# Which tiles of a head pair are turned on TensorE: three and three, or two and four

## Chip, cores and metric

The kernel runs on one core of a Trainium2 chip. The metric is the device time of one execution in microseconds; several executions are timed and their median is given. One further execution is profiled, and its trace is what the prediction reads.

## What is computed

Three layers follow each other, on 2 batches of 768 rows:

1. Attention with 8 heads of width 64. Query and key rows are hashed into 64 buckets by the signs of 6 projections; a score counts only where the buckets agree.
2. A mixing layer, `u = x + (x^T U V)^T` along the rows, then `u + relu(u w_ch1) w_ch2` with widths 512, 2048, 512.
3. Four causal attention experts of width 64, of which each row takes the best two by a gate.

```python
scores = np.where(mask, scale * q @ k.T, -1e9)
attn = softmax(scores); x = attn @ v            # layer 1, per head
u = x + (x.T @ U @ V).T
x = u + np.maximum(u @ w_ch1, 0) @ w_ch2        # layer 2
```

## The kernel before

All three layers are cut into tiles of 128 rows. The change touches layer 1 of batch 0 alone. There the 8 heads are worked off as 4 pairs (pair 0 to 3 below), each pair as two heads of six row tiles; the twelve tiles of a pair are numbered 0 to 11 here, 0 to 5 in the first head, 6 to 11 in the second (`a1_head`). Each tile goes through these steps:

- TensorE makes 128 x 768 scores in PSUM (L606, L611); VectorE copies them out as `P32` with their least value (L617); ScalarE takes the exponential with the row sum (L526, or L575 in the other mode).
- Then the 128 x 768 weights must be turned, so that TensorE can multiply them with the values, and there are two ways. In mode `AP` (`softmax_split`) ScalarE writes a half-precision copy (L528), GpSimd writes the remainder (L534), and the SyncE queue issues one DMA transposition of both halves into the buffer `PT` (L628); TensorE then makes 18 half-precision multiplications (L538 to L540). In mode `FAV` (`softmax_f32`) TensorE turns the float32 weights itself, six blocks in two halves (L581); ScalarE copies one half to SBUF (L586) and VectorE the other (L588), and six float32 multiplications follow, which the trace shows as 12 passes (L590). No DMA takes part.
- When all six tiles of a head have been multiplied, VectorE scales the result into `xn` (L639). The result lies in one PSUM buffer (`po`, tag `pv`, one buffer), so a second head's first product waits for that.

`A1_MODES[b][p]` is the list of modes of a pair; tile `NT * j + t` takes entry `(NT * j + t) % len(list)`. `P32`, `PT` and the half-precision buffer `HL` are rings of five buffers in batch 0. Tiles of batch 1 are all `AP` in pair 0, `AP` and `AV` in turn after that.

What lies around it in the same stretch: while a pair runs, the next pair is prepared (`a1_prep`: GpSimd makes `KN` and `KL`, L409 and L414; the SyncE queue issues three transpositions `AQ`, `AK`, `KT`, L407 to L418, and copies `BQ`, `BK`, L419, L421; the signs follow six tiles later, with four small DMAs, L446, L447); the pair after that is loaded (L381); the weights of layer 2 are loaded and split in 512-column units (L278, then L189 to L195 on VectorE, L281 on ScalarE, L282 and L283 on GpSimd); and the pair before goes through the row mixing of layer 2 (`x_stage_a` to `x_stage_c`, L657 to L683), from which the multiplications of layer 2 (L734, L754) start once batch 0 is complete.

All DMAs are issued from one queue, SyncE's, in order. The order on each engine is not written by hand: a planner places the instructions by priorities (the order of the program, moved by `sooner`) and by a time model of its own.

Of the kernel before, what the change touches and what calls it, by code (L numbers as in the profile page):

```python
# [22 lines left out]
def kernel(  # L23
# [28 lines left out]
    NP = H // 2  # L52
# [8 lines left out]
    CLIP = 8e9  # L61
    WPOOL = True
    A1_MODES = (
        [("AP", "FAV")] * NP,
        [("AP",)] + [("AP", "AV")] * (NP - 1),
    )
    A2_MODES = ("AV", "VP")
# [1137 lines left out]
```

## Time and profile before

| | us |
|---|---|
| median of 3 executions | 636.69 (635.64 to 643.04) |
| profiled execution, its own time | 635.59 |
| its span, first to last instruction | 633.8 |
| TensorE matmul busy | 579.1 (91%) |
| VectorE, ScalarE, GpSimd busy | 422.7, 348.5, 232.1 |

The profiled execution's own time is the one to add to; 1.8 us of it lie outside the span. Busy time is an average over stretches with different limits: batch 0 of layer 1 fills about 18 to 161 us, batch 1 of layer 1 up to about 365 us with layer 2 beside it, and the rest is layers 2 and 3.

### The profile page before, as it was taken

What the parts mean: (1) busy time and instruction counts of PE and PEld (TensorE: products, weight loads), DVE (VectorE), ACT (ScalarE), POOL (GpSimd) and SP (SyncE); (2) the same over time, 40 slices, a digit from 0 to 9 for tenths busy, and PEclk for the clock granted to TensorE, in tenths of its full rate; (3) what the DMA queues carried; (4) which work ended last, traced back from release to release, by engine and by line L of the source; (5) the groups of instructions that cost most, each with busy time, mean ns of one, the idle gap of its engine ahead of it and who ended that gap; (6) DMA issues with size and microseconds to landing.
All of it is one profiled execution on the core that took longest, in us unless ns stands there. A gap on an engine that the chain in (4) does not pass through costs nothing.

```text
span 633.8 us, 16209 instructions
## 1 busy us (share of the span) xinstructions
PE 579.1 (91%) x6498; PEld 477.0 (75%) x6498; DVE 422.7 (67%) x1029; ACT 348.5 (55%) x744; POOL 232.1 (37%) x218
## 2 busy tenths in 40 slices
PE   5698888978798799989999999999999999998995
PEld 3376866757577589875888898878887888997963
DVE  6989696988877863674876555583784435465295
ACT  4769485775786652673776543462453413344273
POOL 4738777686897662231432101020040000002021
PEclk9679797889889999999999999999999999999998
DMA  8799999999989999597587602242263102016064
GB/s 234 140 218 215 243 211 244 227 228 269 219 182 251 231 178 172 101 200 114 108 130 121 101 20 50 38 84 72 46 114 67 34 15 39 27 35 109 23 107 109
DMA packets 228029, 84.36 MB, mean 133 GB/s; under 512 B 207057, under 2 KB 223473, under 8 KB 227953
## 3 DMA queue, kind: packets, MB, share of 16 engines
q1 hardware_dynamic: 227952, 83.32, 65.4%
q8 instruction: 51, 0.84, 0.6%
q14 instruction: 26, 0.20, 0.1%
HBM read 29.11 MB, written 3.15 MB: 51 GB/s over the span
## 4 chain that ended last, share of the span: by engine, by line
PE 59%; DMA 14%; DVE 7%; POOL 7%; ACT 6%; issue 5%; SPq 1%; POOLq 0%; DVEq 0%; ACTq 0%
PE px L754 18%; PE ph L734 12%; DMA PT<-HL 8%; PE po L590 3%; POOL HL L534 3%; PE pq L805 3%; PE s L908 2%; PE pk L805 2%; PE pz L1040 2%; PE pv L837 2%; ACT HL L528 2%; DVE P L617 2%; ACT P L526 2%; DMA more_hT<-more_W 2%; DMA more_hT<-HL 2%
## 5 line engine op out<-in xcount | busy, mean ns | idle before, releaser
L534 POOL TENSOR_TENSOR HL<-P,HL 128x768 f16<-128x768 f32 (+5 forms) x62 | 88.7, 1432 | 323.2 <-DVE HL L530 148.7
L734 PE MATMUL ph<-U,W 128*128 128x256 f16 (+1 forms) x1344 | 145.1, 258 | 1.7 <-DVE hT L736 1.1
L754 PE MATMUL px<-hT,W 128*128 128x256 f16 (+1 forms) x1344 | 146.1, 258 | 0.1
L734 PEld LDWEIGHTS <-W 128*128 128x128 f16 x1344 | 114.2, 98 | 17.1 <-issue 2.4
L754 PEld LDWEIGHTS <-W 128*128 128x128 f16 x1344 | 115.0, 98 | 14.3 <-issue 2.0
L526 ACT ACTIVATE P<-P,m 128x768 f32<-128x768 f32 (+5 forms) x109 | 88.7, 814 | 56.0 <-DVE P L916 28.7
L617 DVE TENSOR_SCALAR_CACHE_REDUCE P<-sc 128x768 f32<-128x768 f32 x76 | 71.9, 950 | 12.8 <-PE sc L611 8.4
L736 DVE SCALAR_TENSOR_TENSOR hT<-ph,hT 128x256 f16<-128x256 f32 (+1 forms) x112 | 42.6, 382 | 45.6 <-ACT hT L735 44.9
L528 ACT ACTIVATE HL<-P 128x768 f16<-128x768 f32 (+5 forms) x80 | 60.5, 758 | 17.6 <-DMA PT<-HL 14.8
L735 ACT ACTIVATE hT<-ph 128x256 f16<-128x256 f32 (+1 forms) x112 | 38.7, 347 | 51.3 <-PE ph L734 47.8
L538 PEld LDWEIGHTS <-PT 128*128 128x128 f16 x516 | 47.8, 99 | 23.8 <-DMA PT<-HL 20.1
L606 PE MATMUL sc<-AK,AQ 128*128 128x512 f16 x192 | 50.0, 341 | 9.3 <-DVE P L617 6.5
L538 PE MATMUL po<-V,PT 128*128 128x64 f16 x372 | 45.7, 195 | 11.5 <-DMA PT<-HL 10.6
L611 PE MATMUL sc<-BK,BQ 88*128 88x512 f16 x192 | 49.9, 340 | 0.0
L539 PEld LDWEIGHTS <-PT 128*128 128x128 f16 x516 | 47.5, 99 | 1.5 <-issue 0.2
L540 PEld LDWEIGHTS <-PT 128*128 128x128 f16 x516 | 47.4, 99 | 0.4
L540 PE MATMUL po<-V,PT 128*128 128x64 f16 x372 | 45.7, 195 | 0.0
L539 PE MATMUL po<-V,PT 128*128 128x64 f16 x372 | 45.2, 195 | 0.0
L534 DVE TENSOR_TENSOR HL<-P,HL 128x768 f16<-128x768 f32 (+5 forms) x42 | 32.3, 769 | 15.4 <-ACT HL L528 14.8
L916 DVE TENSOR_SCALAR_CACHE_REDUCE P<-s 128x128 f32<-128x128 f32 (+5 forms) x48 | 29.5, 618 | 10.9 <-PE s L913 10.6
L606 PEld LDWEIGHTS <-AQ 128*128 128x128 f16 x192 | 18.0, 105 | 17.8 <-issue 13.2
L611 PEld LDWEIGHTS <-BQ 88*128 88x128 f16 x192 | 19.5, 102 | 13.9 <-issue 2.1
(240 smaller groups left out, 1186.7 us busy)
## 6 DMA issues: line engine op xcount, KB each, us to landing
w<-in_moe_w_ch_dram SPq DMA_DIRECT2D x16, 512.0 KB
wx<-in_moe_w_ch_dram SPq DMA_DIRECT2D x16, 512.0 KB
qn<-in_q_dram SPq DMA_DIRECT2D x16, 192.0 KB
kn<-in_k_dram SPq DMA_DIRECT2D x16, 192.0 KB
vn<-in_v_dram SPq DMA_DIRECT2D x16, 192.0 KB
out_dram<-o SPq DMA_DIRECT2D x12, 256.0 KB
PT<-HL SPq DMA_TRANSPOSE x101
BQ<-AQ SPq DMA_DIRECT2D x7, 192.0 KB
```

The source lines that it names most:

```text
L526: nc.scalar.activation(P32, P32, AF.Exp, bias=m, scale=-1.0, accum_out=ssum)
L528: nc.scalar.activation(HL[:, 0], P32, AF.Copy)
L534: eng.tensor_tensor(HL[:, 1], P32, HL[:, 0], op=ALU.subtract)
L538: nc.tensor.matmul(o, PT[:, t, :], vh(t), start=(t == 0), stop=False)
L539: nc.tensor.matmul(o, PT[:, t, :], vl(t), start=False, stop=False)
L540: nc.tensor.matmul(o, PT[:, nk + t, :], vh(t), start=False, stop=(t == nk - 1))
L606: nc.tensor.matmul(ps[:, c0 : c0 + cn], aq[:, t, :], ak[:, c0 : c0 + cn], start=True, stop=False,)
L611: nc.tensor.matmul(ps[:, c0 : c0 + cn], bq[:, t, :], bk[:, c0 : c0 + cn], start=False, stop=True,)
L617: nc.vector.tensor_scalar(P32, ps[:, 0:S], CLIP, None, op0=ALU.min, op1=ALU.min, accum_out=m)
L734: nc.tensor.matmul(ph, w, u, start=(i == 0), stop=(i == len(ops) - 1))
L736: nc.vector.scalar_tensor_tensor(hT[1][:, ft, :], ph, 0.0, hT[0][:, ft, :], op0=ALU.max, op1=ALU.subtract)
L754: nc.tensor.matmul(po, w, u, start=(i == 0), stop=(i == len(ops) - 1))
```

## The change

Batch 0's list of modes gets twelve entries in place of two. Before, tiles 1, 3, 5 (first head) and 7, 9, 11 (second head) are `FAV`; after, tiles 2, 5 and 6, 8, 9, 11. Tiles 1, 3 and 7 change from `FAV` to `AP`, tiles 2, 6 and 8 from `AP` to `FAV`. It applies to all four pairs of batch 0; batch 1 stays.

```diff
     A1_MODES = (
-        [("AP", "FAV")] * NP,
+        [("AP", "AP", "FAV") * 2 + ("FAV", "AP", "FAV") * 2] * NP,
         [("AP",)] + [("AP", "AV")] * (NP - 1),
     )
```

## Rows read from the trace of the kernel before

**Rows 1.** The page: TensorE's busy time, granted clock and DMA share in 40 slices.

```profile
PE 579.1 (91%) x6498; PEld 477.0 (75%) x6498; DVE 422.7 (67%) x1029; ACT 348.5 (55%) x744; POOL 232.1 (37%) x218
...
PEclk9679797889889999999999999999999999999998
DMA  8799999999989999597587602242263102016064
```

**Rows 2.** Windows: busy time of each engine, clock, DMA share; pair 2, then layers 2 and 3.

```profile
84.00:122.00 38.00, 33.24 (x336) 27.23 (x334) 30.55 (x63) 26.87 (x52) 27.80 (x25) 0.87 1.10 228
...
365.00:634.00 269.00, 257.24 (x3022) 220.52 (x3020) 149.99 (x492) 111.76 (x307) 28.76 (x29) 0.99 0.29 58
```

**Rows 3.** Groups of instructions by line and form: count, busy us, mean ns.

```profile
L534 POOL TENSOR_TENSOR HL<-P,HL 128x768 f16<-128x768 f32 x42 | 69.5, 1656 | 97.5 <-ACT HL L528 89.7 <-DVE ss L1013 3.1 <-DVE mx L869 2.9
L528 ACT ACTIVATE HL<-P 128x768 f16<-128x768 f32 x60 | 50.2, 838 | 16.7 <-DMA PT<-HL 14.8 <-DMA more_hT<-HL 1.0
...
L588 DVE COPY PT<-tp 128x384 f32<-128x384 f32 x14 | 7.7, 548 | 2.6 <-PE tp L581 2.6
L586 ACT ACTIVATE PT<-tp 128x384 f32<-128x384 f32 x14 | 6.6, 473 | 0.6 <-PE tp L581 0.6
```

**Rows 4.** Chain of waits, in order of time, pair 2: start us, us, what.

```profile
97.87 4.96 DMA PT<-HL
...
106.34 0.05 PE po L538
...
107.31 2.61 PE po L590 x12
109.92 1.28 PE tp L581 x6
...
121.43 1.37 PE po L590 x12
```

**Rows 5.** Timeline of SyncE's queue, end of pair 1 to end of pair 3.

```profile
81.31 0.39 SPq L278 DMA_DIRECT2D w<-in_moe_w_ch_dram  x1
82.41 1.47 SPq L628 DMA_TRANSPOSE more_hT<-more_W  x1
...
88.31 1.92 SPq L407 DMA_TRANSPOSE AQ<-QN  x1
...
97.87 1.47 SPq L628 DMA_TRANSPOSE PT<-HL  x1
...
101.23 1.75 SPq L628 DMA_TRANSPOSE more_hT<-HL  x1
...
104.91 3.37 SPq L628 DMA_TRANSPOSE PT<-HL  x1
...
113.72 1.50 SPq L628 DMA_TRANSPOSE more_hT<-more_W  x1
115.33 0.81 SPq L278 DMA_DIRECT2D wx<-in_moe_w_ch_dram  x1
119.06 2.41 SPq L628 DMA_TRANSPOSE PT<-more_W  x1
...
158.01 3.72 SPq L407 DMA_TRANSPOSE AQ<-QN  x1
161.83 1.29 SPq L628 DMA_TRANSPOSE PT<-HL  x1
```

**Rows 6.** Timeline of VectorE, pair 2: tiles 7 and 8 leave PSUM.

```profile
101.48 0.94 DVE L617 TENSOR_SCALAR_CACHE_REDUCE more_W<-sc 128x768 f32<-128x768 f32 x1
...
114.41 0.96 DVE L617 TENSOR_SCALAR_CACHE_REDUCE P<-sc 128x768 f32<-128x768 f32 x1 [0.96 <-PE sc L611]
```

**Rows 7.** Windows of 2 us, pair 2: columns as in rows 2.

```profile
100.00:102.00 2.00, 0.20 (x2) 0.00 (x0) 2.00 (x5) 1.72 (x4) 2.00 (x2) 1.00 1.21 176
...
104.00:106.00 2.00, 2.00 (x14) 2.00 (x14) 0.00 (x0) 0.00 (x0) 2.00 (x2) 0.50 1.17 285
```

**Rows 8.** Timeline of GpSimd, pair 2: the remainder of tile 8.

```profile
117.39 1.64 POOL L534 TENSOR_TENSOR more_W<-P,more_W 128x768 f16<-128x768 f32 x1 [0.80 <-ACT more_W L528]
```

## Prediction

> **What bounds the kernel now.** I read the page first. TensorE is busy 91% of the span, but that is an average: the granted clock falls again and again in the first third, and the DMA engines are taken nine tenths or more in most slices there [rows 1]. Next the windows by stage. In pair 2 no engine is full: TensorE 33.2 of 38 us, part of it at half clock, VectorE 30.6, GpSimd 27.8, while the DMA share is 1.10, over one, so transfers queue behind each other. From 365 us on TensorE works 257 of 269 us and the DMA share is 0.29 [rows 2]. So batch 0 is a stretch of transfers and waits, everything behind it is TensorE's, and since the multiplications of layer 2 start when batch 0 is done, a microsecond won or lost in batch 0 reaches the end whole, unless the planner finds room for it.
>
> Then the timelines of one pair, pair 2. Its transpositions on SyncE's queue stand at 97.87, 101.23, 104.91, 113.72, 119.06 and a sixth later, for tiles 0, 2, 4, 6, 8, 10; ahead of the first stand the three of the next pair's preparation, from 88.31 on [rows 5]. TensorE runs dry while it waits for the first: 0.20 us busy in 100 to 102. Right after it the clock is 0.50 [rows 7], that is 1.2 GHz in place of 2.4, and the backlog is worked off slowly: the chain has a tile's 12 passes at 2.61 us there, against 1.37 us later [rows 4]. Tile 8's scores stand behind that backlog in TensorE's order, so VectorE, which took tile 7 at 101.48, gets tile 8 at 114.41 [rows 6]. This stop of 13 us in the middle of the pair is what the change can touch; pairs 1 and 3 show the same pattern.
>
> **The change part by part.** Counts first. Six tiles of a pair are turned by DMA and six on TensorE before and after, so no engine's work changes: the sum of removed and added instructions is nothing, for all four pairs. What is left is where they stand. Per pair the first head gets one DMA tile more and one TensorE tile less, the second head the reverse.
>
> One tile changed from TensorE to DMA, in the first head:
> - GpSimd gets a remainder of 1.66 us, ScalarE a copy of 0.84 for one of 0.47, so 0.37 more; VectorE loses a copy of 0.55 [rows 3].
> - TensorE at half clock loses 12 passes of 2.61 us and six turns of 1.28, and gets 18 multiplications at 0.05, so 3.89 less 0.90, or 3.0 us; at full clock about half, 1.5 us [rows 4].
> - SyncE's queue gets a transposition. Two of them follow each other at 3.36 and 3.68 us, the loads between them included [rows 5]; the chain shows 4.96 us from issue to the waiting multiplication [rows 4].
>
> The second head has each of these with the other sign. GpSimd, ScalarE and VectorE have gaps in either head (27.8, 26.9 and 30.6 of 38 us [rows 2]), so I cost them at nothing. That cover is thinnest on GpSimd, which is full in both windows of [rows 7] (2.00 of 2.00 us); without it the 1.66 us would show in each pair.
>
> Two things are left that can show.
>
> First, **the middle of the pair**. Tile 4, the last DMA tile of the first head, goes from third to fourth place among the pair's transpositions. The first head's result must be scaled out before the second head's products may start (one PSUM buffer), so they wait for it. The cost is between nothing and one pitch: nothing if the planner puts the fourth right behind the third and the half-clock backlog hides it (TensorE has 1.5 to 3.0 us less to do by then); 3.7 us if all of it is waited for. If the fourth kept its present slot, it would be 8.8 us behind the third (113.72 less 104.91 [rows 5]), but what lies between is loads and small copies that the planner is free to put behind it. I take half a pitch, 1.85 us.
>
> Second, **the fifth transposition**. It belongs to tile 8 now and to tile 7 after. In pair 2 the queue is free at 116.14 (115.33 and 0.81) and issues it at 119.06 [rows 5], the moment the remainder of tile 8 is done (117.39 and 1.64 [rows 8]). Tile 7 was scored 13 us earlier [rows 6], so its transposition would not wait. The gain is 2.92 us in pair 2, but 0.71 in pair 1 (81.70 to 82.41) and 0.10 in pair 3 (161.73 to 161.83 [rows 5]): mean 1.2 us, ends 0 and 2.9. After the fifth as many tiles are served as before (tiles up to 9), and after the sixth all, so nothing else is won or lost at the end of a pair.
>
> Net 1.85 less 1.2, or 0.65 us later per pair. Pair 0 is prepared in another way and I leave it out; three pairs give 2.0 us. 635.59 and 2.0 is 637.6 us against the profiled execution's own time. That execution lies 1.1 us under the median of the three runs shown, so I give **638 us**.
>
> The clock needs a word of its own. In this trace each dry spell of TensorE is followed by a stretch at half clock [rows 7]. The Trainium skill says the same in "TensorE: Matmul & The Clock Gate", section "HAM oscillation — how this bites in real kernels": bursts that wait for a transfer between them lose the clock and run at half rate. By that rule the change works against itself, since it puts four waits for transfers in the first head in place of three; the trace agrees as far as it goes, and the rival below prices it.
>
> **Rivals.** *Slower: the fourth transposition is waited for in full, and TensorE goes cold longer.* Place: the multiplications of tile 4, before the second head's first product. Price: one pitch of 3.7 us and no gain at the fifth, in four pairs 14.8 us, so 650 us; it decides where TensorE's first-head work (two TensorE tiles in place of three) no longer bridges the time between transpositions. For it: TensorE is already dry ahead of the first one. Against it: after that spell TensorE is the late one, not the queue, until tile 8's scores.
>
> *Faster: the second head no longer waits.* With two DMA tiles instead of three there, the fifth transposition issues 2.9 us sooner in every pair and the fourth hides in the backlog: four times 2.9 is 11.7, so 624 us. If in addition the half-clock stretch were shortened by one tile's difference (2.61 less 1.37, 1.2 us), it would be 5 us less again, 619. For it: the 13 us stop is mainly TensorE's backlog at half clock. Against it: two of the three pairs show a wait of under 1 us at the fifth.
>
> *The planner moves other work.* Its order over all engines depends on the modes, and the change may shift weight loads or the mixing step by a transposition's pitch, in either direction: one pitch of 3.7 us, so 632 or 640. That the change does nothing is excluded; each tile reads its mode from the list.
>
> **How the numbers follow.** The forecast with the planner's shifts (630 to 645 us) gets 0.78, the slower rival 0.12, the faster 0.10. The range, from 628 to 648, leaves out the outer half of both rivals. A change of 2% is about what a measurement of this kernel tells from none; that is 12.7 us, so faster means under 624.0 and slower over 649.4. The faster rival stands at the first bound and the slower just over the second, so each gives about half its chance, and a little falls to worse shifts: faster 0.06, within 2% 0.86, slower 0.08.
>
> **What would show it.** In the changed trace the transpositions of a pair belong to tiles 0, 1, 3, 4, 7, 10. Right: tile 4's is issued later in the pair than 20 us after tile 0's score, the fifth follows the fourth without a wait for GpSimd, and the pair's length stays within 2 us of 38. Wrong to the slow side: TensorE's half-clock stretch, 10 us in pair 2 now, grows. Wrong to the fast side: the stop between tiles 7 and 8 shrinks by several us and layer 2's first multiplication comes earlier. The forecast fails altogether if the end moves while layer 2 starts at the same time, since then the cause lies behind batch 0.

## The result, and the profile after

The changed kernel takes 641.14 us (median of 20 runs, 637.07 to 642.86) where the kernel before took 635.75 (20 runs, 630.91 to 643.04) on the same chip: ratio 1.0086, 95% interval 1.0066 to 1.0105. So it is slower by some 5 us, less than the 2% that the chances were given for, within the range and on the forecast's side, but not where the forecast put it. The profiled execution took 638.57 us, 3.0 more than that of before, and is the one that the rows show; of the 5.4 us between the medians they can account for these 3.0.

The page and the windows first, columns as in [rows 1, 2]; the second window is the first head of batch 1.

```profile
PE 577.7 (91%) x6498; PEld 469.7 (74%) x6498; DVE 421.6 (66%) x1029; ACT 347.7 (55%) x744; POOL 232.8 (37%) x218
...
84.00:122.00 38.00, 32.83 (x345) 25.91 (x344) 32.80 (x63) 28.74 (x53) 29.23 (x26) 0.96 1.05 228
171.79:197.17 25.38, 23.07 (x250) 16.39 (x249) 16.74 (x31) 17.45 (x34) 18.28 (x17) 0.80 0.95 189
```

Against [rows 1] TensorE's multiplications have 1.4 us less, the other engines differ by about 1 us at most. Pair 2 even runs at 0.96 of the clock where it ran at 0.87 [rows 2]. No work was added, so the end must have moved by order.

Where it moved is seen from VectorE's scaling of each head's result (L639). Its timeline in the changed kernel, pair 3 and batch 1's first head.

```profile
157.30 0.56 DVE L639 TENSOR_TENSOR xn<-po,r 128x384 f32<-128x384 f32 x1 [1.06 <-PE po L590]
...
171.79 0.56 DVE L639 TENSOR_TENSOR xn<-po,r 128x384 f32<-128x384 f32 x1 [2.46 <-PE po L590]
...
197.17 0.56 DVE L639 TENSOR_TENSOR xn<-po,r 128x384 f32<-128x384 f32 x1 [3.35 <-PE po L540]
```

The same line in both traces, with the time since the head before:

| result (L639) | before, us | after, us | head took before | after | difference |
|---|---|---|---|---|---|
| pair 0, second head | 59.73 | 56.76 | | | -2.97 |
| pair 1, first | 80.11 | 84.39 | 20.38 | 27.63 | +7.25 |
| pair 1, second | 94.70 | 97.05 | 14.59 | 12.66 | -1.93 |
| pair 2, first | 117.22 | 118.28 | 22.52 | 21.23 | -1.29 |
| pair 2, second | 133.31 | 131.78 | 16.09 | 13.50 | -2.59 |
| pair 3, first | 150.65 | 157.30 | 17.34 | 25.52 | +8.18 |
| pair 3, second | 173.15 | 171.79 | 22.50 | 14.49 | -8.01 |
| batch 1, first head | 190.98 | 197.17 | 17.83 | 25.38 | +7.55 |

Over pairs 1 to 3 first heads lose 14.1 us and second heads win 12.5; pair 0 wins 3.0, and batch 0 ends 1.4 us earlier. Layer 2's first multiplication is 1.2 us earlier too (177.35 to 176.13). (Batch 0 ends with pair 3's second head, at 173.15 us in the kernel before, and not at about 161.) Then one head of batch 1, whose modes were not touched, takes 7.6 us more. From there on nothing else is lost on balance: layer 3 begins at 371.6 us instead of 367.0, and from it to the end of the span it is 265.3 us against 266.8.

One trace of each kernel doesn't carry all of this. In three versions below (signs_whole, small_loads_after, mixing_later) the order on every engine is that of the changed kernel through batch 0. Batch 0 ends in them at 171.4, 175.4 and 175.1 us. In small_loads_before, which has the order of the kernel before up to some 160 us, pair 3's first result comes at 147.5 us instead of 150.65. So batch 0 moves by 3 to 4 us from one execution to the next, and that it ends 1.4 us earlier is not shown. What all four traces of the new order show is the shape: the first heads of pairs 1 and 3 take 26.2 to 27.6 and 25.3 to 25.7 us (20.4 and 17.3 before), that of pair 2 20.9 to 21.3 (22.5), every second head is shorter, and batch 1's first result comes at 197.2 to 198.9 us instead of 191.0.

SyncE's queue tells what stands between the transpositions of that head. The changed kernel, from the end of pair 2 to the middle of batch 1's first pair, columns as in [rows 5]:

```profile
117.37 0.51 SPq L381 DMA_DIRECT2D vn<-in_v_dram  x1
118.01 2.06 SPq L628 DMA_TRANSPOSE more_hT<-more_W  x1
...
136.72 1.49 SPq L628 DMA_TRANSPOSE more_hT<-HL  x1
...
147.45 3.35 SPq L628 DMA_TRANSPOSE more_hT<-more_W  x1
150.85 0.57 SPq L381 DMA_DIRECT2D vn<-in_v_dram  x1
...
151.99 0.80 SPq L446 DMA_DIRECT2D BQ<-SG  x1
...
155.88 1.81 SPq L628 DMA_TRANSPOSE PT<-HL  x1
...
162.82 2.16 SPq L628 DMA_TRANSPOSE more_hT<-HL  x1
...
168.28 1.21 SPq L418 DMA_TRANSPOSE KT<-KL  x1
...
170.25 1.59 SPq L628 DMA_TRANSPOSE PT<-HL  x1
171.94 1.73 SPq L421 DMA_DIRECT2D BK<-KT  x2
173.72 0.59 SPq L381 DMA_DIRECT2D qn<-in_q_dram  x1
174.41 0.56 SPq L278 DMA_DIRECT2D wx<-in_moe_w_ch_dram  x1
175.15 3.24 SPq L628 DMA_TRANSPOSE PT<-HL  x1
178.43 0.57 SPq L381 DMA_DIRECT2D kn<-in_k_dram  x1
...
189.98 1.76 SPq L628 DMA_TRANSPOSE PT<-HL  x1
```

And the kernel before in the rows that [rows 5] leave out, from pair 3's fourth transposition on:

```profile
149.19 2.42 SPq L628 DMA_TRANSPOSE PT<-more_W  x1
...
153.24 1.22 SPq L418 DMA_TRANSPOSE KT<-KL  x1
154.59 0.50 SPq L381 DMA_DIRECT2D qn<-in_q_dram  x1
155.19 1.13 SPq L278 DMA_DIRECT2D wx<-in_moe_w_ch_dram  x1
156.75 0.69 SPq L381 DMA_DIRECT2D kn<-in_k_dram  x1
157.50 0.41 SPq L381 DMA_DIRECT2D qn<-in_q_dram  x1
...
170.13 3.59 SPq L628 DMA_TRANSPOSE PT<-HL  x2
173.77 0.89 SPq L278 DMA_DIRECT2D w<-in_moe_w_ch_dram  x1
174.83 2.39 SPq L628 DMA_TRANSPOSE PT<-HL  x1
...
183.50 3.32 SPq L628 DMA_TRANSPOSE PT<-HL  x2
```

In the kernel before, pair 3's stop between the fourth transposition and the fifth (149.19 to 161.83, since tile 8 is scored late) holds five instructions that the changed kernel issues later: `KT`, `qn`, `wx`, `kn`, `qn`. In the changed kernel the first head's four transpositions follow each other closely (136.72 to 147.45, 10.7 us, where four took 15.9), a value load and the four small copies that lay among them come behind the fourth, and the fifth belongs to tile 7 and follows at once. `KT` now stands just ahead of the first transposition of batch 1's first head (168.28), so that its two copies `BK`, which were ahead too, fall among the transpositions with the other four. The head's first transposition is issued at 170.25 us, as before at 170.13; the sixth at 189.98 instead of 185.02 (the second of the pair of rows at 183.50).

### The profile page after: what moved, and what is told of

It is laid out like the page before. It is cut to its first block, busy times and chain, and to the rows that moved or that the text cites. A ratio compares the mean times of both kernels' runs of the same rounds, so it can differ in the third digit from the quotient of the medians.

```text
span 636.9 us, 16203 instructions
## 1 busy us (share of the span) xinstructions
PE 577.7 (91%) x6498; PEld 469.7 (74%) x6498; DVE 421.6 (66%) x1029; ACT 347.7 (55%) x744; POOL 232.8 (37%) x218
## 4 chain that ended last, share of the span: by engine, by line
PE 54%; DMA 17%; POOL 11%; DVE 6%; issue 5%; ACT 4%; SPq 2%; POOLq 0%; DVEq 0%; ACTq 0%
PE ph L734 14%; PE px L754 13%; DMA PT<-HL 10%; POOL HL L534 4%; PE s L908 3%; PE pq L805 3%; PE pk L805 2%; PE pv L837 2%; PE po L590 2%; PE pz L1040 2%; POOL W L283 2%; PE sg L436 2%; PE sc L611 1%; DMA more_hT<-HL 1%; DMA more_hT<-more_W 1%
## 5 line engine op out<-in xcount | busy, mean ns | idle before, releaser
L734 PE MATMUL ph<-U,W 128*128 128x256 f16 (+1 forms) x1344 | 147.6, 259 | 1.4 <-ACT U L209 0.8
L734 PEld LDWEIGHTS <-W 128*128 128x128 f16 x1344 | 114.8, 99 | 19.1 <-issue 4.0
L538 PEld LDWEIGHTS <-PT 128*128 128x128 f16 x516 | 47.4, 98 | 28.5 <-DMA PT<-HL 21.9
L606 PE MATMUL sc<-AK,AQ 128*128 128x512 f16 x192 | 51.7, 351 | 9.6 <-DVE P L617 5.9
L611 PE MATMUL sc<-BK,BQ 88*128 88x512 f16 x192 | 52.3, 355 | 0.0
L606 PEld LDWEIGHTS <-AQ 128*128 128x128 f16 x192 | 18.5, 106 | 18.2 <-issue 14.4
```

Of the source, the lines that this page charges most:

```text
L538: nc.tensor.matmul(o, PT[:, t, :], vh(t), start=(t == 0), stop=False)
L606: nc.tensor.matmul(ps[:, c0 : c0 + cn], aq[:, t, :], ak[:, c0 : c0 + cn], start=True, stop=False,)
L611: nc.tensor.matmul(ps[:, c0 : c0 + cn], bq[:, t, :], bk[:, c0 : c0 + cn], start=False, stop=True,)
L734: nc.tensor.matmul(ph, w, u, start=(i == 0), stop=(i == len(ops) - 1))
```

## The experiments

All kernels were timed in five rounds beside the kernel before on the same chip, whose median there lay between 632.8 and 636.0 us; ratios are against it, with their 95% interval. Four theories are on trial, named as in the expectations. **A**: batch 0 hands on transfers (1.7 MB by 200 us), and batch 1's first pair pays for them. **B**: the signs of batch 1's pair 2, which the new order scatters behind layer 2's multiplications. **C**: TensorE at half clock at 185 us. **M**: TensorE's order in batch 1's first head.

**Signs in one piece.** The changed kernel with these 16 multiplications of L436 kept together:

```diff
+            with tc.tile_critical() if (b, p) == (1, 2) else nullcontext():
+                for c0, cn in halves(S):
...
```

> The changed kernel, with the 16 sign multiplications of batch 1, pair 2, kept together in TensorE's order; in the changed kernel they stand one by one between layer 2's passes and take 7.3 us there (250.0 to 257.3 us of its trace). Theory A (batch 0 hands a backlog of transfers to batch 1, and the loss is that delay): no change, ratio to the kernel before 1.007 to 1.010. Theory B (the loss is the scattered signs): 3.6 to 3.9 us back, ratio 1.002 to 1.003, and layer 2's first block of the trace no longer thinned out at 250 us.

642.74 us, ratio 1.0099 (1.0060 to 1.0138). The signs stand together at 253.8 us, and nothing is gained. B falls; the ratio is the one that A expected.

**The change in some pairs only** (pairs 0 to 2, then pair 3), and its mirror image, with four DMA tiles in the second head, each as an edit of the changed kernel's line:

```diff
-        [("AP", "AP", "FAV") * 2 + ("FAV", "AP", "FAV") * 2] * NP,
+        [("AP", "AP", "FAV") * 2 + ("FAV", "AP", "FAV") * 2] * (NP - 1) + [("AP", "FAV")],
...
+        [("AP", "FAV")] * (NP - 1) + [("AP", "AP", "FAV") * 2 + ("FAV", "AP", "FAV") * 2],
...
+        [("FAV", "AP", "FAV") * 2 + ("AP", "AP", "FAV") * 2] * NP,
```

> The change in pairs 0 to 2 only. By the built order, the signs of batch 1, pair 2, still stand scattered behind layer 2's block of 192 passes. Theory A: the changed trace is 0.5 MB behind at 120 us and 1.8 MB at 180 us, so pairs 0 to 2 make a third of the backlog: ratio 1.002 to 1.004. Theory B: the scattering is still there, ratio 1.006 to 1.009.

640.62 us, ratio 1.0083 (1.0049 to 1.0117).

> The change in pair 3 only. By the built order the signs of batch 1, pair 2, stand ahead of layer 2's block and together, as in the kernel before. Theory A: two thirds of the backlog, ratio 1.005 to 1.007. Theory B: ratio 0.999 to 1.002.

641.74 us, ratio 1.0063 (1.0029 to 1.0096).

> The reverse of the change: four tiles of the first head and two of the second are turned on TensorE. By the built order the signs of batch 1, pair 2, stand ahead and together. Theory A: the queue has less to do in the first head, so no backlog, ratio 0.995 to 1.000. Theory B: ratio 0.998 to 1.002. If the first-head wait of the prediction were the cause, the middle of the pair would shorten and the ratio be 0.99 or less.

636.81 us, ratio 1.0031 (1.0005 to 1.0058). The loss isn't shared out over the pairs: three pairs alone make as much as all four, the fourth alone some three quarters (the intervals overlap), and the mirror image a third. A missed pairs 0 to 2 and the mirror image and met pair 3 alone; that the loss adds up over the pairs falls. In pairs_0_to_2 pair 3 keeps its modes, yet its stop shrinks to 4.7 us (152.76 to 157.44), and batch 1's first head has the queue of the changed kernel.

Pair 3 alone also speaks against C as the whole cause. The window of batch 1's first head there, then in the kernel before:

```profile
171.98:196.72 24.74, 19.36 (x233) 14.42 (x232) 16.09 (x30) 17.84 (x33) 19.25 (x16) 0.86 1.00 202
```

```profile
173.15:190.98 17.83, 17.09 (x220) 12.72 (x219) 13.60 (x27) 14.43 (x26) 16.46 (x14) 0.83 0.86 179
```

The head takes 24.7 us at no lower a clock. In the changed kernel it is a little colder, 0.80: worked out from these shares, some 10 us at half clock in place of 6. Four such microseconds cost about 2 us by estimate, so C can be a part there.

**Fewer transfers.** Three weight units aren't loaded; the unit before them is split again in their place. In the changed kernel, then in the kernel before:

```diff
+        SKIP = ("w1_1_3", "w1_3_3", "w2_0_1")
...
-        nc.sync.dma_start(o, src)
+        if name in SKIP:
+            st = last_st[0]
+        else:
+            nc.sync.dma_start(o, src)
+        last_st[0] = st
```

> The changed kernel, but three of the weight units of layer 2 (w1_1_3, w1_3_3, w2_0_1; 0.5 MB each) are not loaded: the unit before them is split once more in their place, so that part of the second matrix's result is a different one. Every other instruction stays; 1.5 MB of transfers are gone from the stretch 120 to 220 us. Theory A (batch 0 hands about 1.7 MB of transfers on to the first pair of batch 1, whose transpositions then stand in a queue of transfers): the 1.5 MB are nearly the arrears, so the loss goes: 634 to 638 us, ratio 0.997 to 1.003, first result of batch 1 back from 197 towards 192 us. Rival C (the loss comes from the half-clock stretch of TensorE that the new order has at 185 us, and transfers only follow): nothing changes for TensorE, 640 to 642 us, ratio 1.007 to 1.01.

639.30 us, ratio 1.0054 (1.0023 to 1.0085).

> The kernel before with the same three units not loaded (the unit before them split once more in their place), so that the run above is measured against a kernel with as few transfers. Theory A: the kernel before has no arrears in the first pair of batch 1, but its transfers queue there as well (DMA share above one); it gains less than the changed kernel does, 631 to 636 us, ratio 0.993 to 1.000. Rival C: the same gain as the changed kernel, nothing, ratio 0.998 to 1.002.

634.97 us, ratio 0.9990 (0.9955 to 1.0025). 1.5 MB less in each leave 0.0064 of the 0.0086 between them; the intervals are too wide to say that the loss shrank. The changed kernel's 1.0054 misses both A's range and C's, and batch 1's first result comes at 204.3 us, not back towards 192: the planner put thirteen other instructions between the head's transpositions, so this edit changed the order too.

**The loads of batch 1's pair 2 earlier**, by a priority of 150, then 400, in the changed kernel:

```diff
-                later(1 + i, fn)
+                up = 150 if (b, p) == (1, 2) else 0
+                later(1 + i, lambda fn=fn, up=up: sooner(up, fn))
```

> The changed kernel with nothing left out; the six loads of batch 1's pair 2 are put earlier in the order, four of them ahead of or between the transpositions of pair 3's second head, where the kernel before has three of them and has one preparation's transposition besides. Theory A: four of six loads (0.8 MB of 1.7 MB) are gone from the arrears, so half of the loss goes: 637 to 639.5 us, ratio 1.002 to 1.006, provided that batch 0 doesn't get longer by them. Rival C: no change, 640 to 642 us.

643.96 us, ratio 1.0127 (1.0077 to 1.0177).

> As loads_before_pair, but the four loads of queries and keys stand ahead of pair 3's fifth transposition by a whole block, and the two of values ahead of the first pair's second transposition. Theory A: arrears smaller by the same 0.8 MB or a little more, 636 to 639 us, ratio 1.000 to 1.005; if the loads only push batch 0's own transpositions back, the gain is lost again in batch 0, whose last result then comes later than 172 us. Rival C: no change, 640 to 642 us.

641.55 us, ratio 1.0131 (1.0100 to 1.0162). Both miss A's numbers; only the second lies within C's 640 to 642 us. The loads do stand earlier, but pair 3's last result comes at 178.8 and 174.6 us, against 171.4 to 175.4 in the four traces of the new order: with 150 they lengthen batch 0, which the expectations had allowed for; with 400 that is not clear.

**The same loads at a sixth of their bytes**, in the changed kernel and in the kernel before:

```diff
+        if (b, p) == (1, 2):
+            nats[b, p] = kept[0]
+            todo = [(kept[0][i][:, r, :], s_[:, 0:1, :]) for i, r, s_ in (
+                (0, slice(0, 1), todo[0][1]), (1, slice(0, 1), todo[1][1]),
...
```

> The changed kernel with its order of SyncE's queue kept around the border of the batches, but each of the six loads for batch 1's pair 2 brings one tile of rows instead of six (the rest of that pair's rows are those of the pair before), so 0.98 MB are gone from between the transpositions of batch 1's first pair. Theory A (the first pair of batch 1 is longer since these loads, which the kernel before has partly in the stop of pair 3, stand between its transpositions): most of the loss goes, 635.5 to 638 us, ratio 0.999 to 1.004, first result of batch 1 from 197 back to 191 to 194 us. Rival C (TensorE at half clock around 185 us, or work on another engine that the new order has moved): 640 to 642 us, ratio 1.006 to 1.010.

639.93 us, ratio 1.0119 (1.0074 to 1.0164).

> The kernel before with the same six loads cut to a sixth; the planner draws two weight units forward into the room. Theory A: these loads cost it little, since three of them stand in the stop of pair 3 where SyncE's queue has nothing else: 633 to 636 us, ratio 0.996 to 1.001. Rival C: as the changed kernel, no difference beyond 0.002.

641.33 us, ratio 1.0129 (1.0090 to 1.0169). Both miss A's ranges, and by their ratios C's. A as a matter of bytes alone falls: 0.98 MB less in the changed kernel bring nothing at the end, and the kernel before loses as much as the change does although it moves less. SyncE's queue in that last kernel, batch 1's first head:

```profile
167.87 7.37 SPq L640 DMA_TRANSPOSE PT<-HL  x3
175.29 1.34 SPq L393 DMA_DIRECT2D vn<-in_v_dram  x2
...
181.99 0.52 SPq L278 DMA_DIRECT2D wx<-in_moe_w_ch_dram  x1
182.62 4.22 SPq L640 DMA_TRANSPOSE PT<-HL  x2
186.90 0.82 SPq L278 DMA_DIRECT2D w<-in_moe_w_ch_dram  x1
187.81 0.49 SPq L278 DMA_DIRECT2D wx<-in_moe_w_ch_dram  x1
188.39 0.46 SPq L278 DMA_DIRECT2D w<-in_moe_w_ch_dram  x1
188.95 4.64 SPq L640 DMA_TRANSPOSE PT<-HL  x1
```

The planner took the shorter loads as an invitation to put weight units and the sign copies between the transpositions, eleven instructions in all. Batch 0 ended 4.8 us earlier than in the kernel before (168.38 against 173.15; some 3 us of that is the scatter named above), and batch 1's first result came 8.3 us later (199.24 against 190.98). But most of that is made up in the next head: batch 1's second result is 1.3 us late (218.67 against 217.34). A long first head and the loss at the end aren't the same thing.

**The preparation ahead.** The changed kernel with the last steps of `KT` and three loads put forward, so that the head has as few instructions between its transpositions as before:

```diff
+        sooner(60 if (b, p) == (1, 1) else 0, low_keys)
...
+                up = 120 if (b, p) == (1, 2) and i < 3 else 0
+                later(1 + i, lambda fn=fn, up=up: sooner(up, fn))
```

Here `low_keys` makes `KL` and issues `KT`.

> The changed kernel, nothing left out. For the preparation of batch 1's pair 1 the remainders of the keys and their transposition stand earlier, and so do the first three loads of pair 2; in SyncE's queue they lie between pair 3's fifth and sixth transposition, and batch 1's first pair has about the same transfers between its transpositions as in the kernel before. Theory A as an order: first result of batch 1 at 191 to 195 us, 636 to 639 us, ratio 1.000 to 1.005. Theory A as a matter of throughput (what is drawn forward lengthens pair 3, since its stop is gone and there is no free time left to fill): last result of pair 3 later than 174 us, 640 to 644 us, ratio 1.006 to 1.012. Rival C: 640 to 642 us with pair 3 unchanged at 172 us.

640.54 us, ratio 1.0121 (1.0078 to 1.0164). Its queue:

```profile
162.57 4.28 SPq L631 DMA_TRANSPOSE more_hT<-HL  x1
...
174.50 1.50 SPq L631 DMA_TRANSPOSE PT<-HL  x1
...
189.55 1.77 SPq L631 DMA_TRANSPOSE PT<-HL  x1
```

The six transpositions again take 15.0 us, as in the kernel before. But the first is issued at 174.50 instead of 170.25, so the sixth is no earlier: 189.55 and 189.98. A as an order (636 to 639 us) missed. The time is that of A as a matter of throughput, and as much that of C; pair 3's last result, at 173.0 us, lies between the marks that were to tell them apart (later than 174, unchanged at 172).

**TensorE's order.** In the kernels that lose, 48 to 72 multiplications of layer 2 stand ahead of the first head's last product, in the kernel before 36, in the mirror image 24. One edit brings the changed kernel to 24 and leaves SyncE's order in this head alone:

```diff
-        later(LAGC, lambda: sooner(XP[p == NP - 1], lambda: x_stage_c(b, p, xs, T)))
+        later(LAGC + 1 * ((b, p) == (0, NP - 1)), lambda: sooner(XP[p == NP - 1], lambda: x_stage_c(b, p, xs, T)))
```

> The changed kernel with the last step of pair 3's row mixing (layer 2's input) called one tile later. SyncE's order stays the same up to the middle of batch 1's first pair; in TensorE's order 24 multiplications of layer 2 stand ahead of the first head's last product instead of 60. Theory M (TensorE is the late engine in batch 1's first head, and the multiplications of layer 2 that the planner put into it make it long): the head takes 18 to 21 us instead of 25, first result of batch 1 at 190 to 193 us, 635 to 638 us, ratio 0.999 to 1.004. Theory A (transfers between the transpositions, or any other cause on SyncE's queue): no change, first result at 196 to 198 us, 640 to 642 us, ratio 1.006 to 1.011.

645.30 us, ratio 1.0103 (1.0048 to 1.0158). M's numbers (a head of 18 to 21 us, 635 to 638 us) miss, and as the whole cause M falls; A's ratio and first result (197.9 us) came about. The window of the head and the ends of its queue's stretch:

```profile
175.06:197.94 22.88, 18.09 (x210) 12.78 (x209) 15.80 (x30) 15.78 (x29) 16.37 (x15) 0.78 1.05 205
```

```profile
173.50 1.57 SPq L628 DMA_TRANSPOSE PT<-HL  x1
...
193.29 1.81 SPq L628 DMA_TRANSPOSE PT<-HL  x1
```

TensorE has 5 us less to do in the head and waits, 4.2 us in one piece; the transpositions still take 19.8 us. Here they set the head, at 22.9 us. In the changed kernel itself TensorE is the late one at its end:

```profile
185.99 0.23 PE L538 MATMUL po<-V,PT 128*128 128x64 f16 x1 [0.90 <-DMA PT<-HL]
...
188.21 4.74 PE L734 MATMUL ph<-U,W 128*128 128x256 f16 x24
192.78 0.19 PE L538 MATMUL po<-V,PT 128*128 128x64 f16 x1
```

From 185.99 us to the head's last product it doesn't pause, with 24 of layer 2's multiplications among it. Of the head's 25.4 us it is busy for 23.1 (17.1 of 17.8 before), and only 0.9 us is a wait for a transposition. From the sixth transposition's issue to the head's result it takes 7.2 us, in mixing_later 4.7. So two limits lie close together in this head, the transpositions and what the planner gave TensorE to do; mixing_later lifts the second and meets the first.

**All kernels side by side.** Read from SyncE's timeline of each: the instructions other than transpositions of weights that stand between the first and the sixth of batch 1's first head, and the time between the two.

| kernel | others between | first issued, us | first to sixth, us | ratio |
|---|---|---|---|---|
| before | 4 | 170.1 | 14.9 | 1 |
| before_fewer_weights | 4 | 166.6 | 14.9 | 0.9990 |
| preparation_ahead | 4 | 174.5 | 15.0 | 1.0121 |
| four_then_two | 5 | 172.7 | 15.1 | 1.0031 |
| loads_before_pair | 8 | 176.8 | 18.8 | 1.0127 |
| loads_far_ahead | 8 | 172.8 | 19.1 | 1.0131 |
| small_loads_after | 9 | 174.0 | 18.2 | 1.0119 |
| pair_3_alone | 9 | 172.1 | 19.0 | 1.0063 |
| signs_whole | 9 | 171.2 | 19.4 | 1.0099 |
| pairs_0_to_2 | 9 | 170.6 | 19.4 | 1.0083 |
| changed kernel | 9 | 170.3 | 19.7 | 1.0086 |
| mixing_later | 9 | 173.5 | 19.8 | 1.0103 |
| small_loads_before | 11 | 167.9 | 21.1 | 1.0129 |
| after_fewer_weights | 13 | 171.9 | 19.6 | 1.0054 |

Up to eleven, each instruction more goes with 0.9 us more for the head's transpositions ((19.7 - 14.9) / 5 = 0.96; (21.1 - 14.9) / 7 = 0.89); with thirteen that fails (19.6). It is not all their own issue. From the kernel before to the changed one the others' issue grows by 3.2 us (2.6 to 5.9), that of the first five transpositions by 3.0 (9.5 to 12.5), and smaller gaps give 1.4 back. The others' part goes by their number, 0.6 to 0.8 us each in all these kernels: with a sixth of the bytes the same nine take 6.0 us. The transpositions' own part is smaller in both versions of the changed kernel that move fewer bytes (10.8 us in small_loads_after, 9.4 in after_fewer_weights). The ratio doesn't follow the spacing: preparation_ahead has the spacing of the kernel before and 1.0121, after_fewer_weights 19.6 us and 1.0054.

## Why the prediction came out as it did

**The number** was right, 638 us and a range from 628 to 648 against 641.14, and so was the sign. That was luck in good part: the 2.0 us were to be lost in three pairs of batch 0, and the one loss that stands out of the traces lies behind it, in a head that the prediction didn't cost. (Its own sum, 637.6 and 1.1, is 638.7 and not 638.)

**No work is added.** Right: GpSimd's busy time went from 232.1 to 232.8 us, ScalarE's from 348.5 to 347.7, VectorE's from 422.7 to 421.6, and the groups of [rows 3] keep their counts and means:

```profile
L534 POOL TENSOR_TENSOR HL<-P,HL 128x768 f16<-128x768 f32 x42 | 69.4, 1655 | 95.8 <-ACT HL L528 87.2 <-DVE cmp L866 3.1 <-DVE ss L1013 3.1
...
L588 DVE COPY PT<-tp 128x384 f32<-128x384 f32 x14 | 7.7, 551 | 0.2 <-PE tp L581 0.2
```

**The middle of the pair.** The mechanism is there, its size was too small: from the first to the last DMA tile of the first head the queue takes 4.6, 4.4 and 2.8 us more in pairs 1 to 3 (in pair 2 11.4 us, 98.84 to 110.28, against 7.0, 97.87 to 104.91), a pitch and not half of one. The heads themselves take 4.7 us more on the mean (+7.25, -1.29, +8.18), where I took 1.85 and at most 3.7; in pairs 1 and 3 the first transposition also comes 3.6 and 5.0 us later after the result before it. Tile 4's transposition is issued at 110.28 us in pair 2, 23.3 us after tile 0's scores left PSUM (86.98), as forecast.

**The fifth transposition** no longer waits for GpSimd: 117.37 and 0.51, then 118.01 us. The second heads win 4.2 us on the mean (1.93, 2.59, 8.01), where I took 1.2 and at most 2.9. In pair 2 tiles 7 and 8 leave PSUM 6.8 us apart (104.53 and 111.37) instead of 12.9 [rows 6]. Both terms were off by a factor of 2.5 to 3.5 and nearly cancel: 1.6 us for three pairs (-0.7 to 2.4 in the other three traces of this order), forecast 2.0. That they cancel is luck. That the pair's length would stay within 2 us of 38 didn't hold: pair 2 takes 34.7 us, pair 1 40.3.

**Pair 0**, which I left out, wins 3.0 us here and 0.2 to 2.6 in the other three traces.

**The step that failed** is "nothing else is won or lost at the end of a pair", with the loads and small copies "that the planner is free to put behind" the fourth transposition, which I costed at nothing. They were put behind it, and what they pushed out stands in batch 1's first head, which takes 25.4 us instead of 17.8. The stop that I took for lost time was, in pair 3, where SyncE issued work for batch 1. With it fails the premise that what lies behind batch 0 only follows it: TensorE needs 7.1 us more there (below), and [rows 1] have the DMA engines taken some nine tenths up to 253 us, far into batch 1. The prediction's last test had it: the end moves while layer 2 starts at about the same time (176.1 us, and 175.5 to 179.9 in the other three traces, against 177.4), so the forecast failed by it and the cause lies, at least in the main, behind batch 0.

**The colder rival** didn't come about: pair 2's clock rose from 0.87 to 0.96, and the first heads of pairs 1 to 3, with four waits for transfers in place of three, ran at 0.88, 0.93 and 0.87, where they had 0.83, 0.77 and 0.80. The waits became more, but the longest in these pairs shorter (2.95 us before, 2.12 after). The Trainium skill, "TensorE: Matmul & The Clock Gate", section "HAM oscillation — how this bites in real kernels", has bursts with waits for a transfer between them run at half rate. That one wait more makes the head colder was my own reading of it, and batch 0 doesn't bear it out. Nor does each dry spell end in half clock, as the prediction has it: in the kernel before TensorE stands still for 1.40 us from 152.53, and the clock stays at 1.00. In batch 1's first head the clock does fall behind waits: TensorE stands still for 0.80, 0.61 and 0.90 us between 182 and 186 us, only the last time for a transposition, and this window behind it, columns as in [rows 7], lies at half the clock, 1.2 GHz.

```profile
190.00:192.00 2.00, 2.00 (x11) 1.43 (x10) 0.89 (x3) 2.00 (x4) 1.96 (x1) 0.50 0.92 204
```

**The planner's rival** named the right thing, moved weight loads and small transfers, and its price of one pitch (3.7 us, 640 us) was the nearest to the result; I had it inside the forecast and not as its cause, and its place, batch 1, was not named.

**What is shown and what isn't.** Shown is that batch 1's first head is longer in the changed kernel, and that the spacing of its transpositions follows the order of SyncE's queue: two edits moved the number of other instructions (9 to 4, 4 to 11), and the spacing went with it (19.7 to 15.0, 14.9 to 21.1). Not shown is that this spacing costs the 5 us at the end. The edit that undid it lost the time ahead of the first transposition, and no version here is faster than the kernel before.

TensorE's account is the other half. Batch 0, then from its end to layer 3, in the kernel before, then the same in the changed one:

```profile
18.00:173.15 155.15, 130.41 (x1231) 103.43 (x1230) 131.21 (x252) 111.97 (x206) 114.39 (x100) 0.85 1.05 222
173.15:366.96 193.81, 183.33 (x2208) 149.41 (x2207) 129.35 (x246) 117.42 (x220) 81.98 (x64) 0.98 0.84 156
```

```profile
18.00:171.79 153.79, 122.94 (x1225) 94.89 (x1225) 128.01 (x247) 109.42 (x203) 111.55 (x98) 0.89 1.01 213
171.79:371.61 199.82, 190.40 (x2212) 151.83 (x2211) 132.29 (x250) 119.00 (x225) 85.55 (x67) 0.97 0.84 159
```

In batch 0 TensorE is busy 7.5 us less, at a higher clock, and idle 6.1 us more, so batch 0 is only 1.4 us shorter. Behind it TensorE is busy 7.1 us more for nearly the same multiplications (2212 and 2208), and idle 1.1 us less. In the sum of the page the two cancel. Why it is busy longer there is only in part known: the half clock is some 2 us of it by the estimate above, and the signs of L436 are busy 3.8 us longer (7.7 to 11.5, partly beside other multiplications), though keeping them together gained nothing.

Not settled either is why SyncE's queue doesn't even out. From pair 2's sixth transposition to the sixth of batch 1 SyncE issues 46 instructions in either kernel, in 57.7 us before (127.30 to 185.02) and 64.3 after (125.65 to 189.98), the gaps between them 6.4 and 5.8 us of it. The issue of a weights' transposition is itself longer, 2.4 us against 1.9 (28.5 and 23.0 us for twelve). That it takes longer because the transfers ahead of it haven't drained would fit the two versions with fewer bytes; no run tests it by itself.

## What to carry to other kernels

A stop on a critical queue may be the only place where the next stage's transfers fit: before you remove it, list what is issued in it and say where that goes. When all DMAs leave from one queue, count its instructions between two that matter, and not only their bytes. A change that only reorders should be followed past its own stage, to the first milestone that is later than it was; a sum of busy time over the whole span can hide that one stage gained what another lost.

## What was not expected of the hardware

A small load takes as much of the queue as a large one: a load of keys of batch 1's pair 2 takes 0.57 us of SyncE's queue with 192 KB (178.43 in the changed kernel) and 0.58 with 32 KB (181.34 in small_loads_after). The five loads among the head's transpositions at a sixth of their bytes took 1.5 us off it, all of it from the issue of the transpositions themselves. And 16 small multiplications of L436 (32 columns wide) that stand one by one between full-width ones are spread from 250.0 to 257.3 us, where the same 16 together take 1.5 us (253.79 to 255.26 in signs_whole); keeping them together gained nothing at the end.
